# Soft-capped attention and a gated convolution on one core: sums and products with v in four groups of 32 TensorE columns, and a new order of every engine's work

## The chip, the cores and the metric

The kernel runs on one core of a Trainium2 chip. Its engines are TensorE (PE; its weight loads are listed apart as PEld), VectorE (DVE), ScalarE (ACT), GpSimd (POOL) and SyncE (SP), which here issues all DMAs. The metric is the time of one execution on the device in microseconds (us). Lower is better.

## The reference, cut to what matters

```python
# q, k, v: (8, 12, 448, 64); cap = 30
scores = (1 / sqrt(64)) * matmul(q, k.T)
scores = cap * tanh(scores / cap)
attn = exp(scores - max(scores))
attn = attn / (sum(attn) + 1e-9)
x = matmul(attn, v)                 # heads side by side: (8, 448, 768)
# gate: causal depthwise convolution of 5 taps over the sequence, per channel
gate = sigmoid(sum_k conv_w[k] * xp[:, k:k+448, :])
out = (gate * (x @ w_val)) @ w_out  # w_val, w_out: 768 x 768
```

conv_w, w_val and w_out arrive as float64, the rest as float32.

## The kernel before, in words

The 96 heads are taken as 48 pairs p; six pairs make a batch b. A pair's two heads lie on the two halves of the 128 partitions. Names of steps are those of the functions; names of tiles in brackets are those that the profile prints.

For each pair, SyncE loads q and k in blocks (qn, kn) and v (vn), and VectorE turns q and k into 64 channels by 448 positions (qt, kt; "tq", "tk"). From pair 13 on q and k are also split into a high and a low half (qh, ql, kh, kl: casts on ScalarE, subtractions on VectorE), and three matmuls of the halves take the place of one fp32 matmul. `scores` makes, for one of four chunks i of 112 keys and both heads, 112 keys by 2 x 448 queries (pss, two buffers in PSUM). `tanh` and `exp` on ScalarE make the unnormalised weights from it (pt, six buffers); no maximum is subtracted, since the cap bounds the scores. `add` on VectorE adds the four chunks up (pa): not at all before pair 6, in two pairs of chunks up to pair 10, and to one tile from pair 11 on.

Two steps then use pt. `av` (function attnv) multiplies a chunk with v: for each head 112 keys by 64 columns of v as weights and 448 queries streamed, the first head into PSUM partitions 0 to 63 and the second into 64 to 127 of one bank (psa). `sums` does the same with a tile of ones for weights (psz), so that every one of a head's 64 partitions holds the head's sum for each query. It runs once per chunk before pair 6 (four units), twice for pairs 6 to 10, once from pair 11 on: 24 + 10 + 37 = 71 units. For odd pairs below 6 both banks come from the two buffers of psf.

`turn_sums` transposes psz in 32 x 32 blocks (zt), `recip` takes one column of each block, adds a small guard and makes the reciprocals (rc), `spread` transposes them back over 32 partitions, and `mul` makes x (u, two buffers) from psa and zt. `x_hi` and `x_lo` split x (xh on ScalarE, xl on VectorE). Five `conv` steps make the gate's argument: the first is a scaled copy (on ScalarE below pair 11, on VectorE after), the others VectorE steps that each need the one before.

For each batch `sigmoid` (ScalarE) is applied to the six gates. `val` makes x @ w_val from the halves (three matmuls each, psf), `gate` multiplies, `gated_hi` and `gated_lo` split the result (g_h, g_l), and `out` makes the product with w_out, which `store` copies out of PSUM on ScalarE (osb) and `store_out` sends. In the first two batches the weights are brought from float64 into halves wv and wo, in twelve steps (weight_load, late_load, weight_first on ScalarE, weight_second and weight_third on VectorE).

The order is written out by hand. Every step is entered with a time, in units of one pair, and all are sorted by it; each engine runs its instructions in exactly that order. In the kernel before, the times come from small tables by kind of pair:

```python
"av": (1.10, 1.15, 1.20, 1.25), "sums": (1.28,), "turn_sums": 1.41, "recip": 1.42,
SIG_FIRST, SIG_AT = 6.92, 7.44          # one time for all six sigmoids of a batch
at(p + y, f, p, i)                      # a step of pair p
for _, _, f, a in sorted(events, key=lambda e: e[:2]): f(*a)
```

Tanh and exp are in one of ScalarE's function tables and the sigmoid is in another. The program loads a table (ACT_TABLE_LOAD) where the order goes from the one to the other.

The profile's lines of the kernel before that are spoken of below: scores L326, tanh L334, exp L338, add L348 and L345, av L363, sums L375, turn_sums L383, recip L389 and L390, spread L396, mul L404, x_hi L409, conv L421, L423 and L425, sigmoid L431, val L446 to L448, gate L452, gated_hi L455, out L475 to L477, store L483, turns of q and k L305, splits of weights L140 to L150, weight loads L272 and L280.

Of the kernel before, what the change touches and what calls it, by code (L numbers as in the profile page):

```python
# [7 lines left out]
F32 = mybir.dt.float32  # L8
# [32 lines left out]
STEADY = {  # L41
    "load_q": -1.9,
    "load_k": -1.85,
    "load_v": -0.6,
    "tq": -0.90,
    "tk": -0.85,
    "scores": (0.0, 0.05, 0.62, 0.67),
    "tanh": (0.06, 0.13, 0.68, 0.75),
    "exp": (0.22, 0.29, 0.82, 0.89),
    "add": (0.52, 1.03, 1.06),  # L50
    "av": (1.10, 1.15, 1.20, 1.25),
    "sums": (1.28,),
    "turn_sums": 1.41,
    "recip": 1.42,
    "spread": 1.44,
    "mul": 1.50,
    "x_hi": 1.52,
    "x_lo": 1.58,
    "conv": (1.60, 1.61, 1.64, 1.67, 1.70),
}  # L60

SPLIT = STEADY | {"q_hi": -0.69, "k_hi": -0.68, "q_lo": -0.475, "k_lo": -0.47}
PAIRED = STEADY | {"add": (0.52, 1.03), "sums": (1.28, 1.29)}
EARLY = {
    "load_q": -1.9,
    "load_k": -1.85,
    "load_v": -0.7,
    "tq": -0.72,
    "tk": -0.70,
    "scores": (-0.50, -0.49, 0.10, 0.11),  # L70
    "tanh": (0.0, 0.01, 0.35, 0.36),
    "exp": (0.17, 0.18, 0.52, 0.53),
    "av": (0.28, 0.37, 0.65, 0.80),
    "sums": (0.29, 0.38, 0.66, 0.81),
    "turn_sums": 1.02,
    "recip": 1.03,
    "spread": 1.04,
    "mul": 1.05,
    "x_hi": 1.30,
    "x_lo": 1.34,  # L80
    "conv": (1.31, 1.50, 1.52, 1.54, 1.56),
}

SIXTH = PAIRED | {k: EARLY[k] for k in ("tq", "tk", "scores", "tanh", "exp")} | {"add": (0.38, 0.62)}


TOGETHER = {
    "scores": (0.0, 0.05, 0.31, 0.32),
    "tanh": (0.06, 0.13, 0.34, 0.36),
    "exp": (0.22, 0.29, 0.47, 0.53),  # L90
    "add": (0.52, 0.60, 0.61),
}
NEXT_TOGETHER = {
    "turn_sums": 1.41, "recip": 1.42, "spread": 1.43, "mul": 1.44, "x_hi": 1.45, "x_lo": 1.54,
    "conv": (1.58, 2.16, 2.17, 2.18, 2.19),
}
PREPARE_TOGETHER = {"q_hi": -0.69, "k_hi": -0.68, "q_lo": -0.44, "k_lo": -0.43}

GATE_FIRST = {"x_lo": 1.66, "conv": (1.67, 1.68, 1.69, 1.70, 1.71)}
LATE_X = {"x_lo": 1.76, "conv": (1.78, 1.80, 1.83, 1.86, 1.89)}  # L100
NEARLY, NPAIRED, NPLAIN = 6, 11, 13

VAL_FIRST = (6.50, 6.85, 7.36, 7.74, 8.36, 8.74)
VAL = (6.85, 7.36, 7.74, 8.36, 8.74, 9.36)
SIG_FIRST, SIG_AT = 6.92, 7.44
OUT_EVEN = (9.80, 10.36, 10.74, 11.36, 11.74, 12.36)
OUT_ODD = (9.80, 10.36, 10.74, 10.80, 11.36, 11.74, 11.80, 12.36)
OUT_LATE = (9.80, 10.36, 10.74, 11.74, 12.36, 12.60)
PART = 0.13
KEEP_AT = 10.2  # L110
W_AT = (0.70, 1.70, 2.70, 3.70, 4.70, 5.70, 7.1, 8.035, 9.035, 9.7, 10.4, 11.035)
W_LOAD = -0.5
W_SECOND, W_THIRD, W_THIRD_EARLY = 0.02, 0.05, 0.71
W_FREE = 11.3
CW_LOAD, CW_AT = -0.55, 0.6
EPS = 1e-9
# [13 lines left out]
def float64_split(nc, raw, mid, hi, lo, t):  # L130

    tf = t.bitcast(F32)
    top = raw[..., 1].bitcast(F32)

    def first():
        nc.scalar.activation(tf, top, AF.Copy, scale=2.0 ** -112)  # L140
        nc.scalar.sign(top, top)

    def second():
        nc.vector.tensor_scalar(t, t, 0x0FFFFE00, 3, ALU.bitwise_and, ALU.logical_shift_left)
        nc.vector.tensor_tensor(hi, tf, top, op=ALU.mult)

    def third():
        nc.vector.tensor_scalar(mid, mid, 0x01FFFFFF, None, ALU.bitwise_and)
        nc.vector.tensor_scalar(t, hi.bitcast(I32), -0x00800000, None, ALU.bitwise_and)
        nc.vector.scalar_tensor_tensor(lo, mid, 2.0 ** -36, tf, ALU.mult, ALU.mult)  # L150

    return first, second, third
# [49 lines left out]
def fast_path(tc, io, u2, q, k, v, w_val, conv_w, w_out, out, capt):  # L202
# [20 lines left out]
    ROWS = [slice(j * D, (j + 1) * D) for j in range(2)]  # L223

    with ExitStack() as ctx:
# [24 lines left out]
        ones = cpool.tile([P, D], F32, name="ones")  # L250
# [12 lines left out]
        wstate = {}  # L263
# [11 lines left out]
        def late_load(n):  # L275
# [80 lines left out]
        def attnv(p, i):  # L356
# [5 lines left out]
            for j, r in enumerate(ROWS):  # L362
                nc.tensor.matmul(  # L363
                    st["o"][r, :S], vloads[p][:, j, i], t[:, j], start=(i == 0), stop=(i == NKT - 1)
                )

        def sums(p, i):

            st = state[p]
            n = len(tables[p]["sums"])  # L370
# [3 lines left out]
            for j, r in enumerate(ROWS):  # L374
                nc.tensor.matmul(st["z"][r, :S], ones[:CH], t[:, j], start=(i == 0), stop=(i == n - 1))  # L375
            if i == n - 1:
                vloads.pop(p)

        def turn_sums(p):
# [3 lines left out]
            nc.vector.transpose(st["zt"], st.pop("z")[:, :S])  # L383

        def norm_recip(p):
            st = state[p]
            rc = wk.tile([P, S // BLK], F32, name="rc", bufs=1)
            col = st["zt"].rearrange("p (c e) -> p c e", e=BLK)[:, :, 0]
            nc.vector.tensor_scalar(rc, col, guard, None, ALU.add)  # L389
            nc.vector.reciprocal(rc, rc)  # L390
# [16 lines left out]
        def x_hi(p):  # L407
            xh = wk.tile([P, S], F32R, name="xh", bufs=NXX)
            nc.scalar.copy(xh, gates[p][1][:, PAD:PAD + S])  # L409
# [80 lines left out]
        cw_steps = []  # L490
        events = []
        tables = [EARLY if p < NEARLY else SIXTH if p == NEARLY else PAIRED if p < NPAIRED else STEADY if p < NPLAIN else SPLIT for p in range(NP)]
        for p in range(NPAIRED, NP):
            if p % NPAIR == 0:
                tables[p] = tables[p] | LATE_X

        def together(p):
            return NPLAIN < p < NP and p % NPAIR not in (1, 3)

        for p in range(NPLAIN, NP):  # L500
            if together(p - 1):
                tables[p] = tables[p] | PREPARE_TOGETHER
            if together(p):
                tables[p] = tables[p] | TOGETHER
            if p % NPAIR == 2:
                tables[p] = tables[p] | GATE_FIRST
            if together(p + 1):
                tables[p] = tables[p] | NEXT_TOGETHER

# [13 lines left out]
        for p, table in enumerate(tables):  # L523
            for name, f in steps.items():
                x = table.get(name, ())
                if isinstance(x, tuple):
                    for i, y in enumerate(x):
                        at(p + y, f, p, i)
                else:
                    at(p + x, f, p)  # L530
        for b in range(B):
            t0 = NPAIR * b
# [207 lines left out]
```

## Time and profile before

| | |
|---|---|
| timed runs, median of 3 | 743.75 us (742.98 to 746.29) |
| span of the profiled execution | 739.6 us, first to last instruction |
| TensorE busy | 717.1 us (97%), 3972 matmul records |
| VectorE busy | 593.0 us (80%), 972 instructions |
| ScalarE busy | 534.7 us (72%), 708 instructions |
| GpSimd busy | 9.0 us (1%) |
| DMA | 63.75 MB, mean 86 GB/s |

The profiled execution's own time is its span; the timed runs also hold what lies around it. "Busy" is the time in which at least one of an engine's instructions ran. Matmuls are pipelined and one record's length includes the way through the array, so two records overlap and a busy TensorE isn't TensorE at its peak. Rows of groups read: line, engine, operation, tiles (written <- read), shapes, count | busy us, mean ns of one | idle us of the engine before them, and what ended the idle time. The granted TensorE clock was full (0.998) throughout.

### The profile page before, as it was taken

What the parts mean: (1) busy time and instruction counts of PE and PEld (TensorE: products, weight loads), DVE (VectorE), ACT (ScalarE), POOL (GpSimd) and SP (SyncE); (2) the same over time, 40 slices, a digit from 0 to 9 for tenths busy, and PEclk for the clock granted to TensorE, in tenths of its full rate; (3) what the DMA queues carried; (4) which work ended last, traced back from release to release, by engine and by line L of the source; (5) the groups of instructions that cost most, each with busy time, mean ns of one, the idle gap of its engine ahead of it and who ended that gap; (6) DMA issues with size and microseconds to landing.
All of it is one profiled execution on the core that took longest, in us unless ns stands there. A gap on an engine that the chain in (4) does not pass through costs nothing.

```text
span 739.6 us, 10858 instructions
## 1 busy us (share of the span) xinstructions
PE 717.1 (97%) x3972; PEld 488.8 (66%) x3972; DVE 593.0 (80%) x972; ACT 534.7 (72%) x708; POOL 9.0 (1%) x16
## 2 busy tenths in 40 slices
PE   5999999999999999999999999999999999999997
PEld 2333655556767776686677766757766876676997
DVE  2899999888997789988899669988899778997410
ACT  5899977787876678776957679587787659774311
POOL 0000001000000000000000000000000000000000
PEclk9999999999999999999999999999999999999999
DMA  6998867854223332224331333223322333200001
GB/s 109 223 212 209 202 171 154 225 118 80 39 49 80 74 74 38 61 67 88 57 57 47 88 75 65 39 69 74 73 38 61 70 87 57 51 24 33 23 22 68
DMA packets 241820, 63.75 MB, mean 86 GB/s; under 512 B 228448, under 2 KB 235616, under 8 KB 241760
## 3 DMA queue, kind: packets, MB, share of 16 engines
q1 hardware_dynamic: 241760, 62.98, 38.6%
q8 instruction: 33, 0.54, 0.3%
q14 instruction: 27, 0.22, 0.1%
HBM read 51.94 MB, written 11.01 MB: 85 GB/s over the span
## 4 chain that ended last, share of the span: by engine, by line
PE 52%; DVE 21%; ACT 13%; issue 2%; SPq 1%; DMA 0%; DVEq 0%; ACTq 0%
PE pss L326 9%; PE psf L475 8%; PE psf L477 7%; PE psf L476 7%; DVE gate L425 7%; PE psa L363 6%; PE psf L446 4%; PE psf L447 4%; PE psf L448 4%; ACT pt L334 3%; PE psz L375 3%; DVE pa L348 3%; ACT gate L431 3%; ACT pt L338 2%; DVE pa L345 2%
## 5 line engine op out<-in xcount | busy, mean ns | idle before, releaser
L334 ACT ACTIVATE pt<-pss,rc 112x896 f32<-112x896 f32 x192 | 185.1, 1004 | 39.2 <-PE pss L326 39.2
L338 ACT ACTIVATE pt<-pt,capt 112x896 f32<-112x896 f32 x192 | 189.6, 1041 | 0.1
L363 PE MATMUL psa<-pt,vn 112*64 112x448 f32 x720 | 147.7, 546 | 0.0
L425 DVE SCALAR_TENSOR_TENSOR gate<-u,cw,gate 128x448 f32<-128x448 f32 x192 | 130.6, 680 | 5.7
L475 PE MATMUL psf<-wo,g_h 128*128 128x384 f32 x336 | 115.7, 344 | 0.0
L477 PE MATMUL psf<-wo,g_l 128*128 128x384 f32 x336 | 112.6, 335 | 0.0
L476 PE MATMUL psf<-wo,g_h 128*128 128x384 f32 x336 | 112.4, 335 | 0.0
L446 PE MATMUL psf<-xh,wv 128*128 128x448 f32 x288 | 107.5, 373 | 0.1
L448 PE MATMUL psf<-xl,wv 128*128 128x448 f32 x288 | 104.5, 363 | 0.0
L447 PE MATMUL psf<-xh,wv 128*128 128x448 f32 x288 | 104.4, 362 | 0.0
L363 PEld LDWEIGHTS psa<-pt,vn 112*64 112x64 f32 x720 | 47.8, 136 | 81.4 <-issue 69.7
L348 DVE TENSOR_TENSOR pa<-pt 112x896 f32<-112x896 f32 x84 | 91.1, 1085 | 2.8 <-ACT pt L338 2.8
L483 ACT COPY osb<-psf 128x384 f32<-128x384 f32 x56 | 26.6, 475 | 65.3 <-PE psf L477 63.6
L383 DVE STREAM_TRANSPOSE zt<-psz 128x448 f32<-128x448 f32 x45 | 28.8, 640 | 54.2 <-PE psz L375 54.2
L475 PEld LDWEIGHTS psf<-wo,g_h 128*128 128x128 f32 x336 | 63.1, 188 | 12.3 <-issue 11.3
L446 PEld LDWEIGHTS psf<-xh,wv 128*128 128x128 f32 x288 | 54.0, 187 | 20.2 <-issue 5.4
L476 PEld LDWEIGHTS psf<-wo,g_h 128*128 128x128 f32 x336 | 63.1, 188 | 0.0
L477 PEld LDWEIGHTS psf<-wo,g_l 128*128 128x128 f32 x336 | 63.1, 188 | 0.0
L326 PE MATMUL pss<-qt,kt 64*112 64x448 f32 x208 | 49.6, 594 | 12.3 <-DVE guard L249 7.8
L455 ACT CAST g_h<-gate 128x448 fp32r<-128x448 f32 x48 | 26.3, 562 | 47.2 <-DVE gate L452 47.0
L326 PE MATMUL pss<-qh,kh 64*112 64x448 f32 x280 | 58.0, 408 | 0.0
L409 ACT CAST xh<-u 128x448 fp32r<-128x448 f32 x48 | 27.1, 566 | 42.3 <-DVE u L404 42.0
(74 smaller groups left out, 908.6 us busy)
## 6 DMA issues: line engine op xcount, KB each, us to landing
vn<-in_v_dram SPq DMA_DIRECT2D x96, 112.0 KB, 2.6
out_dram<-osb SPq DMA_DIRECT2D x56, 192.0 KB, 1.9
qn<-in_q_dram SPq DMA_DIRECT2D x188, 56.0 KB, 2.5
kn<-in_k_dram SPq DMA_DIRECT2D x188, 56.0 KB, 2.4
w_raw<-in_moe_w_val_dram SPq DMA_DIRECT2D x12, 384.0 KB, 5.1
w_late<-in_moe_w_val_dram SPq DMA_DIRECT2D x12, 384.0 KB, 4.4
w_raw<-in_moe_w_out_dram SPq DMA_DIRECT2D x12, 384.0 KB, 3.8
w_late<-in_moe_w_out_dram SPq DMA_DIRECT2D x12, 384.0 KB, 4.8
```

The source lines that it names most:

```text
L326: nc.tensor.matmul(ps[:CH, j, :S], st[x][r, c], st[y][r], start=(n == 0), stop=(n == len(parts) - 1))
L334: nc.scalar.activation(st["p", i], st.pop(("s", i)), AF.Tanh, scale=rc8[:CH])
L338: nc.scalar.activation(t, t, AF.Exp, scale=capt[:CH])
L348: nc.vector.tensor_tensor(st["a", i], st["p", 2 * i], st["p", 2 * i + 1], op=ALU.add)
L363: nc.tensor.matmul(st["o"][r, :S], vloads[p][:, j, i], t[:, j], start=(i == 0), stop=(i == NKT - 1))
L425: nc.vector.scalar_tensor_tensor(g, u[:, i:i + S], cw[:, hp, i:i + 1], g, ALU.mult, ALU.add)
L446: nc.tensor.matmul(o, w_h, xh, start=(c == 0), stop=False)
L447: nc.tensor.matmul(o, w_l, xh, start=False, stop=False)
L448: nc.tensor.matmul(o, w_h, xl, start=False, stop=(c == NCC - 1))
L475: nc.tensor.matmul(o, g_h[:, d, s], w_h, start=(d == 0), stop=False)
L476: nc.tensor.matmul(o, g_h[:, d, s], w_l, start=False, stop=False)
L477: nc.tensor.matmul(o, g_l[:, d, s], w_h, start=False, stop=(d == NCC - 1))
```

## The change

1. `av` and `sums` work in four groups of 32 TensorE columns (GROUPS) instead of two of 64. Group g serves head g // 2. In `av` each group takes 32 of the head's 64 columns of v and streams all 448 queries. In `sums` each group streams only half of the head's queries (HQ = 224): the first of a head's two groups the first half, the second the other.
2. `turn_sums` therefore transposes 224 columns instead of 448. `recip` adds the guard to 7 columns (zc) instead of 14, and makes the reciprocals in eight instructions of 32 partitions by 7, each copying one group's half to one of the head's two groups of partitions.
3. The small tables of times are replaced by large ones, one row per pair (PAIRS), batch (BLOCKS) and weight step (WEIGHTS), with a time for every step. Sigmoids get a time each. Which step runs on which engine is unchanged, and so are all other shapes and the number of buffers.

```diff
-STEADY = {
-    "load_q": -1.9,
...
+PAIRS = """
+- - -3.064 -9.09 -5.622 - - - - -4.262 -5.451 -4.05 -3.713 -3.983 -4.666 -3.924 -3.438 -3.329 -3.464 -3.153 -1.811 - -
+  - -2.746 -2.598 -1.455 -0.365 -2.81 -1.83 -1.743 -1.539 -1.354 -1.021 0.536 0.696 1.014 3.151 1.192 1.24 1.616 1.869
...
+    GROUPS = [slice(g * BLK, (g + 1) * BLK) for g in range(P // BLK)]
+    HQ = S * BLK // D
+    HC = HQ // BLK
...
-        ones = cpool.tile([P, D], F32, name="ones")
+        ones = cpool.tile([P, BLK], F32, name="ones")
...
-            for j, r in enumerate(ROWS):
+            for g, r in enumerate(GROUPS):
+                j, d = divmod(g * BLK, D)
                 nc.tensor.matmul(
-                    st["o"][r, :S], vloads[p][:, j, i], t[:, j], start=(i == 0), stop=(i == NKT - 1)
+                    st["o"][r, :S], vloads[p][:, j, i, d:d + BLK], t[:, j], start=(i == 0), stop=(i == NKT - 1)
                 )
...
-            for j, r in enumerate(ROWS):
-                nc.tensor.matmul(st["z"][r, :S], ones[:CH], t[:, j], start=(i == 0), stop=(i == n - 1))
+            for g, r in enumerate(GROUPS):
+                j, d = divmod(g * BLK, D)
+                q = slice(HQ * d // BLK, HQ * (d // BLK + 1))
+                nc.tensor.matmul(st["z"][r, :HQ], ones[:CH], t[:, j, q], start=(i == 0), stop=(i == n - 1))
...
-            nc.vector.transpose(st["zt"], st.pop("z")[:, :S])
+            nc.vector.transpose(st["zt"][:, :HQ], st.pop("z")[:, :HQ])
...
-            col = st["zt"].rearrange("p (c e) -> p c e", e=BLK)[:, :, 0]
-            nc.vector.tensor_scalar(rc, col, guard, None, ALU.add)
-            nc.vector.reciprocal(rc, rc)
+            zc = wk.tile([P, HC], F32, name="zc", bufs=1)
+            col = st["zt"].rearrange("p (c e) -> p c e", e=BLK)[:, :HC, 0]
+            nc.vector.tensor_scalar(zc, col, guard, None, ALU.add)
+            for g, r in enumerate(GROUPS):
+                j, d = divmod(g * BLK, D)
+                for x in range(D // BLK):
+                    nc.vector.reciprocal(rc[r, x * HC:(x + 1) * HC], zc[GROUPS[j * D // BLK + x]])
...
-                at(t0 + sig, sigmoid, b, d)
+                at(t0 + next(row), sigmoid, b, d)
```

What the order makes of it, at three places. Rows are an engine's instructions in the program's order, with x n for equal neighbours; the lines are each kernel's own.

TensorE around the sums of pair 18 (pss scores, psa av, psz sums), first before:

```order
L326 MATMUL pss<-qh,kl 112x448 x2
L326 MATMUL pss<-qh,kh 112x448 x2
L326 MATMUL pss<-ql,kh 112x448 x2
L326 MATMUL pss<-qh,kl 112x448 x2
L363 MATMUL psa<-pt,vn 64x448 x8
L375 MATMUL psz<-pa_2460,ones 64x448 x2
L446 MATMUL psf<-xh,wv 128x448
L447 MATMUL psf<-xh,wv 128x448
```

and now:

```order
L469 MATMUL pss<-qh,kl 112x448 x2
L507 MATMUL psa<-pt,vn 32x448 x8
L523 MATMUL psz<-pa_2831,ones 32x224 x4
L507 MATMUL psa<-pt,vn 32x448 x8
L469 MATMUL pss<-qh,kh 112x448 x2
L469 MATMUL pss<-ql,kh 112x448 x2
```

The sums moved in between two halves of av, and scores follow instead of val. Counted over the whole program, TensorE goes 210 times between full-width, two-row and column-group shapes in either order.

VectorE from the adding-up of pair 18 (L345, now L488) to its x (u), first before:

```order
L345 TENSOR_TENSOR pa_2460<-pa_2460,pa_2472 112x896
L305 STREAM_TRANSPOSE qt<-qn 128x448
L305 STREAM_TRANSPOSE kt<-kn 128x448
L425 SCALAR_TENSOR_TENSOR gate<-u_64,cw,gate 128x448 x4
L383 STREAM_TRANSPOSE zt<-psz 128x448
L389 TENSOR_SCALAR rc<-zt,guard 128x14
L390 RECIPROCAL rc<-rc 128x14
L396 STREAM_TRANSPOSE zt<-rc 128x448
L404 TENSOR_TENSOR u_63<-psa,zt 128x448
```

and now:

```order
L488 TENSOR_TENSOR pa_2831<-pa_2831,pa_2834 112x896
L575 SCALAR_TENSOR_TENSOR gate<-u_63,cw,gate 128x448
L529 STREAM_TRANSPOSE zt<-psz 128x224
L573 TENSOR_SCALAR gate<-u_64,cw 128x448
L536 TENSOR_SCALAR zc<-zt,guard 128x7
L540 RECIPROCAL rc<-zc 32x7 x8
L383 TENSOR_TENSOR xl<-u_63,xh 128x448
L383 TENSOR_TENSOR ql<-qt,qh 128x448
L546 STREAM_TRANSPOSE zt<-rc 128x448
```

Steps of other pairs now stand between the dependent steps, conv steps of two pairs alternate, and u of pair 18 comes seven rows after the last one shown. Of neighbouring conv steps that follow each other directly there are 142 before and 35 now.

ScalarE around sigmoids of the third batch (L431, now L581), first before:

```order
L311 CAST kh<-kt 128x448
L431 ACT_TABLE_LOAD
L431 ACTIVATE gate<-gate 128x448 x6
L409 CAST xh<-u_63 128x448
L334 ACTIVATE pt<-pss,rc_110 112x896
L455 CAST g_h<-gate 128x448 x2
L334 ACTIVATE pt<-pss,rc_110 112x896
L338 ACT_TABLE_LOAD
L338 ACTIVATE pt<-pt,capt 112x896 x2
```

and now:

```order
L581 ACT_TABLE_LOAD
L581 ACTIVATE gate<-gate 128x448
L477 ACTIVATE pt<-pss,rc_110 112x896 x2
L481 ACT_TABLE_LOAD
L481 ACTIVATE pt<-pt,capt 112x896 x3
L559 CAST xh<-u_63 128x448
L454 CAST qh<-qt 128x448
```

The six sigmoids of a batch moved apart, and with them the table loads: beside the one at the start there are 15 in the order before and 57 now. Between the first and the 25th tanh ScalarE has six weight steps, five x_hi and five gate copies before, and five, three and four now.

More of the change, by code (lines that the diff above doesn't have):

```diff
@@ L38 @@
 NPT = 6
-STEADY = {
-    "load_q": -1.9,
[L43 to L97, printed above, removed]
@@ L111 @@
[L111 to L115, printed above, removed]
-EPS = 1e-9
+STEPS = (
+    "load_q load_k load_v tq tk q_hi k_hi q_lo k_lo scores scores scores scores tanh tanh tanh tanh exp exp exp exp "
+    "add add add av av av av sums sums sums sums turn_sums recip spread mul x_hi x_lo conv conv conv conv conv"
+).split()
+PAIRS = """
+- - -3.064 -9.09 -5.622 - - - - -4.262 -5.451 -4.05 -3.713 -3.983 -4.666 -3.924 -3.438 -3.329 -3.464 -3.153 -1.811 - -
+  - -2.746 -2.598 -1.455 -0.365 -2.81 -1.83 -1.743 -1.539 -1.354 -1.021 0.536 0.696 1.014 3.151 1.192 1.24 1.616 1.869
+  2.29
@@ L119, in words, with plan @@
+EPS = 1e-9
+def plan(text):
+    rows = []
+    for line in text.strip("\n").split("\n"):
+        cells = [None if x == "-" else float(x) for x in line.split()]
+        if line.startswith(" "):
+            rows[-1] += cells
+        else:
+            rows.append(cells)
+    return rows
 def words(ap):
@@ L490, in fast_path @@
         cw_steps = []
+        pairs = plan(PAIRS)
+        rounds = [sum(x is not None for n, x in zip(STEPS, row) if n == "sums") for row in pairs]
         events = []
[L492 to L508, printed above, removed]
         def at(when, f, *a):
@@ L522, in fast_path @@
         )
[L523 to L532, printed above, removed]
+        for p, row in enumerate(pairs):
+            seen = {}
+            for name, when in zip(STEPS, row):
+                i = seen[name] = seen.get(name, -1) + 1
+                if when is not None:
+                    at(p + when, steps[name], p, *([i] if STEPS.count(name) > 1 else []))
@@ L552, in fast_path @@
-        for n, t0 in enumerate(W_AT):
-            third = [x + (W_THIRD if x > NEARLY else W_THIRD_EARLY) for x in W_AT]
-            at(W_AT[n - 1] + W_SECOND if n else W_LOAD, weight_load, n)
-            at(third[n - 1] if n else W_LOAD, late_load, n)
-            at(t0, weight_first, n)
-            at(t0 + W_SECOND, weight_second, n)
-            at(third[n], weight_third, n)
+                    at(t0 + next(row), val, b, d, i)
+                for f in (gate, gated_hi, gated_lo):
+                    at(t0 + next(row), f, b, d)
@@ new lines, in fast_path @@
+            for m in range(2 * (NT + b % 2)):
+                for i in range(PARTS):
+                    at(t0 + next(row), out_part, b, m, i)
+                at(t0 + next(row), store, b, m)
+                at(t0 + next(row), store_out, b, m)
+            if b % 2 == 0:
+                at(t0 + next(row), keep_tail)
+        for n, row in enumerate(plan(WEIGHTS)):
+            for f, when in zip((weight_load, late_load, weight_first, weight_second, weight_third), row):
+                at(when, f, n)
```

208 lines of the change are left out of this document (172 added, 36 removed), and 32 rows, old and new, of the table BLOCKS.

## The prediction

> **What bounds the kernel now.** I read the page first, then the groups of instructions, the timeline of TensorE around one row of av and sums steps, the busy times by stage, and last the waits. The span is 739.6 us and TensorE works nearly all of it:
>
> ```profile
> span 739.6 us, 10858 instructions
> ...
> PE 717.1 (97%) x3972; PEld 488.8 (66%) x3972; DVE 593.0 (80%) x972; ACT 534.7 (72%) x708; POOL 9.0 (1%) x16
> ```
>
> Busy shares overlap inside TensorE (matmuls are pipelined), so I price its work by the distance between starts. In the groups each fp32 matmul is two records (768 for the 384 matmuls of av in all), and the sums are 188 + 48 + 48 = 284 records:
>
> ```profile
> L363 PE MATMUL psa<-pt,vn 112*64 112x448 f32 x720 | 147.7, 546 | 0.0
> ...
> L375 PE MATMUL psz<-pa,ones 112*64 112x448 f32 x188 | 43.1, 546 | 3.8 <-DVE pa L345 3.5
> ...
> L375 PE MATMUL psz<-pt,ones 112*64 112x448 f32 x48 | 11.9, 539 | 0.0
> L375 PE MATMUL psf<-pt,ones 112*64 112x448 f32 x48 | 11.8, 539 | 0.0
> ```
>
> In the timeline (start, length, engine, records merged) eight av records take from 102.87 to 104.37, so a pair of records, one for each 64-column half of the array, costs 0.375 us; two passes make a unit (one key chunk, both heads) of 0.75 us, for av and for sums alike:
>
> ```profile
> 102.87 1.67 PE L363 MATMUL psa<-pt,vn 112*64 112x448 f32 x8
> 104.37 1.68 PE L375 MATMUL psz<-pa,ones 112*64 112x448 f32 x8
> 105.98 0.48 PE L446 MATMUL psf<-xh,wv 128*128 128x448 f32 x1
> ```
>
> The sums' eight would end their streaming at 104.37 + 4 x 0.375 = 105.87, and val starts at 105.98: a change of array shape costs 0.11 us.
>
> By stage (start:end, length, then busy us of PE, PEld, DVE, ACT, POOL; below it records of the sums line alone, PE first):
>
> ```profile
> 9.60:73.30 63.70, 61.48 (x290) 20.84 (x290) 51.92 (x93) 60.59 (x72) 0.23 (x1) 1.00 0.92 206
> 73.30:161.60 88.30, 84.77 (x420) 50.90 (x418) 81.11 (x132) 71.61 (x93) 3.14 (x2) 1.00 0.72 178
> 161.60:597.70 436.10, 433.11 (x2502) 308.92 (x2500) 373.35 (x604) 325.15 (x438) 3.46 (x4) 1.00 0.32 65
> 597.70:739.60 141.90, 135.92 (x764) 107.19 (x760) 84.72 (x137) 75.84 (x107) 1.73 (x2) 0.99 0.17 43
> ```
>
> ```profile
> 9.60:73.30 63.70, 22.96 (x94) 7.49 (x96) 1.00 0.92 206
> ```
>
> The first stage holds the first 24 tanh steps. There ScalarE is busy 60.59 of 63.70 us and TensorE 61.48: both are full, and cheaper matmuls alone can't shorten it. After 73.3 us TensorE is busy 84.77 + 433.11 + 135.92 = 653.8 of 666.3 us while VectorE (539.2) and ScalarE (472.6) have room. The waits (us in total, times, longest) say the same: ScalarE waits for scores far more than TensorE for tanh.
>
> ```profile
> ACT pt L334 <- PE pss L326: 39.2, 40, 3.8
> ...
> PE pss L326 <- ACT pt L334: 4.4, 6, 1.6
> PE psz L375 <- DVE pa L345: 3.5, 9, 0.6
> ```
>
> **Part by part.** *Sums over half the queries.* Each of the four column groups streams 224 columns instead of 448, so a pass should take 0.1875 us. Of the 284 sums records 284 - 94 = 190 lie after 73.3 us: 95 passes x 0.1875 = **17.8 us less** on the engine that sets the pace there. The 94 before it are 8.8 us of TensorE, worth nothing by themselves in a stage that ScalarE fills.
>
> *av in four groups.* Four 32-column matmuls replace two of 64, with twice the instructions and the same 448 columns each: 0.375 us a pass if four groups run side by side as two do now, so nothing. The trace shows two streams, not four. How independent they are shows where the second head's v landed late:
>
> ```profile
> 13.71 1.00 PE L363 MATMUL psa<-pt,vn 112*64 112x448 f32 x3
> 14.52 0.54 PE L375 MATMUL psz<-pt,ones 112*64 112x448 f32 x1
> 14.55 0.54 PE L363 MATMUL psa<-pt,vn 112*64 112x448 f32 x1
> ```
>
> One half is already in its sums at 14.52 while the other is still in av at 14.55, and each goes on at its own 0.375: the halves are queues of their own. I take four for the same; the other end is two at a time, doubling av (192 units x 0.75 = +144 us).
>
> *Reciprocals.* Eight of 32x7 replace one of 128x14, and the transpose ahead of them is half as wide. Prices, and how neighbours overlap on VectorE:
>
> ```profile
> L348 DVE TENSOR_TENSOR pa<-pt 112x896 f32<-112x896 f32 x84 | 91.1, 1085 | 2.8 <-ACT pt L338 2.8
> ...
> L404 DVE TENSOR_TENSOR u<-psa,zt 128x448 f32<-128x448 f32 x45 | 28.1, 624 | 1.5
> ...
> L390 DVE RECIPROCAL rc<-rc 128x14 f32<-128x14 f32 x48 | 11.6, 242 | 1.7
> ...
> L243 DVE RECIPROCAL rc<-capt 128x1 f32<-128x1 f32 x1 | 0.2, 165 | 0.7 <-DVE small L704 0.7
> ```
>
> ```profile
> 311.78 0.64 DVE L305 STREAM_TRANSPOSE qt<-qn 128x448 f32<-128x448 f32 x1
> 312.34 0.61 DVE L305 STREAM_TRANSPOSE kt<-kn 128x448 f32<-128x448 f32 x1
> ...
> 313.62 0.23 DVE L389 TENSOR_SCALAR rc<-zt,guard 128x14 f32<-128x14 f32 x1
> 313.89 0.24 DVE L390 RECIPROCAL rc<-rc 128x14 f32<-128x14 f32 x1
> ```
>
> An independent successor starts 0.08 us before its predecessor's end (312.34 against 312.42), a dependent one 0.04 after it (313.89 against 313.85). A reciprocal of seven columns lies between 165 and 242 ns, so eight take 1.32 to 1.94 us, less 7 x 0.08 = 0.56; less the old 0.24, less half a transpose (224 columns at the slope from 624 to 1085 ns for 448: 0.23). That is +0.29 to +0.91 us a pair, 14 to 44 us in all; I take 25, since seven columns are nearer one than fourteen. It is hidden: after 73.3 us VectorE idles 127 us, and the new order places other work between the dependent conv steps (142 neighbouring conv pairs before, 35 now: 107 x 0.12 = 13 us back). Uncovered, it would delay spread and mul, and through psa (one buffer) the next av.
>
> *Sigmoids.* The order sets them singly or in twos and fours between tanh and exp, where six stood together. Every such place costs two table loads: 15 beside the first before, 57 now.
>
> ```profile
> L431 ACT ACT_TABLE_LOAD x8 | 10.3, 1283 | 0.1
> L338 ACT ACT_TABLE_LOAD x7 | 9.0, 1283 | 0.1
> ```
>
> 42 x 1.283 = **53.9 us more on ScalarE**, all after 73.3 us: 472.6 becomes some 530 of 650, still below TensorE. I cost it at nothing, covered by the 39.2 us of tanh waiting for scores and other idle; the rival below has it uncovered.
>
> *First stage.* Between the first and the 25th tanh the row order before has six weight splits, five xh casts and five gate copies; the change has five, three and four. By these rows
>
> ```profile
> L409 ACT CAST xh<-u 128x448 fp32r<-128x448 f32 x48 | 27.1, 566 | 42.3 <-DVE u L404 42.0
> ...
> L141 ACT ACTIVATE w_raw<-w_raw 128x768 f32<-128x768 f32 x12 | 11.3, 943 | 0.4
> L140 ACT ACTIVATE w_t<-w_raw 128x768 f32<-128x768 f32 x12 | 11.1, 921 | 0.9 <-DMA w_raw<-in_moe_w_val_dram 0.9
> ...
> L421 ACT ACTIVATE gate<-u,cw 128x448 f32<-128x448 f32 x11 | 7.3, 666 | 0.0
> ```
>
> 0.943 + 0.921 + 2 x 0.566 + 0.666 = 3.7 us leave, less five overlaps of 0.09: **3.2 us less**. TensorE has then 61.5 - 8.8, so ScalarE stays the limit. By the same count two av units and one sums unit slip behind it: 2 x 0.75 + 0.375 = **1.9 us more** for later. On SyncE the first two weight loads go ahead of pair 1's q and k; these are wanted only after pair 0's four tanh and four exp (8 us of ScalarE), so nothing, at worst a microsecond or two.
>
> *The rest of the order.* 210 changes of array shape before and 210 now by the rows: nothing. Stalls: TensorE's waits for tanh and for the added-up tiles are 4.4 + 3.5 = 7.9 us; an order that spreads work can remove all or, with fuller ScalarE and VectorE, add. I take half off, **4.0 us less**.
>
> Sum: 739.6 - 17.8 - 3.2 + 1.9 - 4.0 = 716.5 us of span. The median of the runs shown, 743.75, lies 4.15 above the profiled span, so **720.5 us**.
>
> **Rivals.**
> *Table loads reach TensorE.* pss has two buffers, so scores i + 2 wait for tanh i; a sigmoid put ahead of that tanh delays it by two loads and itself, 3.1 us. If every load were felt the time is 720.5 + 53.9 = 774. It decides once 23.2 of the 53.9 us (43%) are felt. For it: the third batch has ten loads, and ScalarE's content there comes to 78 us by rows against 85 for TensorE. Against it: tanh mostly waits for scores, not the reverse.
>
> *Four streams are not four times one.* Each per cent that a pass of four slows costs 1.44 us in av; the forecast's gain is gone at 16%, and two at a time gives some 880. For it: no row shows four. Against it: two cost nothing. The Trainium skill's page "TensorE: Matmul & The Clock Gate" (section "Measured speedup vs the span model") lists four row tiles at 3.07 times one, and three column tiles at 2.38. By that, an estimate from the page, a pass takes 1.30 times as long and the time is about 772 us; the trace's own pairs run at a full 2 (two heads in 0.75 us), which speaks against it, and no run here shows four.
>
> *ScalarE and VectorE crowd the steady stage.* Each pair's chain of small reciprocals and the fuller ScalarE give back 10 to 19 us: 730 to 740.
>
> *More is won.* All 666.3 - 653.8 = 12.5 us without a running matmul go, instead of 4: 712; and a third of the 210 x 0.11 = 23 us of shape changes: 704.
>
> **How the numbers follow.** Chances: the forecast (712 to 730) 0.55; more is won (704 to 712) 0.13; crowding (730 to 740) 0.11; table loads 0.12, of which 0.05 end within 0.5% (740 to 747.5, about what a measurement tells from no change) and 0.07 above; four streams 0.09, all slower. Faster is 0.55 + 0.13 + 0.11 = 0.79, same 0.05, slower 0.16. The range 704 to 742 holds the first three and a little of the fourth, 0.80; the forecast's own is 712 to 730.
>
> **What would show it.** Right: sums records at 0.19 us a pass of four groups and av still at 0.375; the 25th tanh near 70 us; batches of six pairs about 2 to 3 us shorter; 57 table loads with tanh still waiting for scores. Wrong: av passes above 0.43 us; TensorE's wait for tanh grown from 4.4 to over 25 us, behind loads; mul late, with av waiting on it.

## The result, and the profile after

The changed kernel takes 733.81 us (median; 733.1 to 735.3) against 745.02 us for the kernel before in the same rounds: a ratio of 0.9865, interval 0.9837 to 0.9893. The gain is 10 to 11 us where 23 were forecast. The profiled span is 731.2 us, 8.4 below the 739.6 of before.

The page after, and then its groups by line and shape (busy us, mean ns, idle before and its releaser):

```profile
span 731.2 us, 13364 instructions
...
PE 699.2 (96%) x5024; PEld 480.1 (66%) x5024; DVE 622.2 (85%) x1308; ACT 593.3 (81%) x750; POOL 7.1 (1%) x16
```

```profile
L507 PE MATMUL psa<-pt,vn 112*32 112x448 f32 x1440 | 152.0, 544 | 2.1 <-DVE u L554 1.7
...
L540 DVE RECIPROCAL rc<-zc 32x7 f32<-32x7 f32 x384 | 73.8, 192 | 6.6
...
L581 ACT ACT_TABLE_LOAD x29 | 37.2, 1283 | 0.4
L481 ACT ACT_TABLE_LOAD x28 | 35.9, 1283 | 0.5
...
L523 PE MATMUL psz<-pa,ones 112*32 112x224 f32 x376 | 26.3, 356 | 4.6 <-DVE pa L488 3.8 <-DVE pa L491 0.7
...
L529 DVE STREAM_TRANSPOSE zt<-psz 128x224 f32<-128x224 f32 x45 | 18.2, 405 | 5.4 <-PE psz L523 5.0
```

The matmuls do what was said of them. In TensorE's timeline (start, length, records merged) 32 av records of four groups, eight passes, are followed by 16 sums records, four passes:

```profile
102.75 3.21 PE L507 MATMUL psa<-pt,vn 112*32 112x448 f32 x32
106.27 0.96 PE L523 MATMUL psz<-pa,ones 112*32 112x224 f32 x16 [0.31 <-DVE pa L491]
107.16 1.76 PE L469 MATMUL pss<-qt,kt 64*112 64x448 f32 x8
```

The last of eight passes ends 3.21 us after the first starts; a record lasts about 0.54 us, so the seven starts between take 2.67, which is 0.38 a pass. Four sums passes take 107.16 - 106.27 = 0.89 us with a change of array shape (0.11) in it, 0.19 to 0.20 a pass. Four column groups run at the pace of two.

By stage, cut at the 1st, 25th, 49th and 169th tanh as before (start:end, length, busy us of PE, PEld, DVE, ACT, POOL; then the granted TensorE clock, the DMA share and GB/s):

```profile
9.80:72.80 63.00, 56.45 (x464) 18.29 (x466) 48.40 (x117) 57.01 (x67) 0.23 (x1) 0.97 0.85 188
72.80:158.70 85.90, 81.67 (x560) 50.28 (x550) 83.14 (x170) 76.50 (x96) 1.46 (x2) 1.00 0.75 186
158.70:588.70 430.00, 422.51 (x3094) 301.67 (x3094) 395.07 (x821) 372.61 (x473) 2.72 (x4) 1.00 0.33 67
588.70:731.20 142.50, 136.67 (x916) 108.79 (x909) 93.69 (x195) 85.70 (x114) 2.30 (x2) 1.00 0.16 42
```

Against the rows of before the stages are 0.7, 2.4, 6.1 and -0.6 us shorter (with 0.2 us more ahead of them). What is new is the third number: VectorE is busy 83.14 of 85.90 us (97%) in the second stage and 395.07 of 430.00 (92%) in the third. VectorE has hardly any room left there, and TensorE's waits show it (engine and line, what it waited for, us, times, longest):

```profile
PE psz L523 <- DVE pa L488: 3.8, 5, 1.1
PE psf L507 <- DMA vn<-in_v_dram: 2.4, 1, 2.4
PE pss L469 <- ACT pt L477: 2.2, 6, 0.7
PE psf L596 <- DVE gate L602: 2.0, 2, 1.2
PE psf L596 <- DVE u L554: 1.7, 1, 1.7
PE psa L507 <- DVE u L554: 1.7, 3, 1.0
PE psf L627 <- DVE g_l L383: 1.6, 2, 1.0
```

In the waits of before, past the start-up, the added-up tiles (pa) were the only work of VectorE that TensorE waited for. Now it waits for u, gate and g_l as well.

### The profile page after: what moved, and what is told of

Its sections match the earlier page's. It is cut to its first block, busy times and chain, and to the rows that moved or that the text cites. A ratio compares the mean times of both kernels' runs of the same rounds, so it can differ in the third digit from the quotient of the medians.

```text
span 731.2 us, 13364 instructions
## 1 busy us (share of the span) xinstructions
PE 699.2 (96%) x5024; PEld 480.1 (66%) x5024; DVE 622.2 (85%) x1308; ACT 593.3 (81%) x750; POOL 7.1 (1%) x16
## 4 chain that ended last, share of the span: by engine, by line
PE 39%; DVE 26%; ACT 10%; issue 3%; DMA 2%; SPq 1%; DVEq 0%; ACTq 0%
PE psa L507 8%; PE pss L469 6%; DVE gate L575 5%; DVE pa L491 5%; PE psf L625 4%; PE psf L627 4%; PE psf L626 4%; ACT pt L481 4%; PE psf L596 3%; PE psf L598 3%; PE psf L597 3%; DVE rc L540 3%; ACT pt L477 2%; DVE pa L488 2%; ACT L481 1%
## 5 line engine op out<-in xcount | busy, mean ns | idle before, releaser
L477 ACT ACTIVATE pt<-pss,rc 112x896 f32<-112x896 f32 x192 | 188.7, 1003 | 51.3 <-PE pss L469 49.6
L481 ACT ACTIVATE pt<-pt,capt 112x896 f32<-112x896 f32 x192 | 194.9, 1042 | 1.3
L507 PE MATMUL psa<-pt,vn 112*32 112x448 f32 x1440 | 152.0, 544 | 2.1 <-DVE u L554 1.7
L575 DVE SCALAR_TENSOR_TENSOR gate<-u,cw,gate 128x448 f32<-128x448 f32 x192 | 127.5, 672 | 1.3
L491 DVE TENSOR_TENSOR pa<-pt 112x896 f32<-112x896 f32 x84 | 90.7, 1089 | 19.9 <-ACT pt L481 19.2
L507 PEld LDWEIGHTS psa<-pt,vn 112*32 112x32 f32 x1440 | 43.3, 110 | 73.2 <-issue 53.6
L540 DVE RECIPROCAL rc<-zc 32x7 f32<-32x7 f32 x384 | 73.8, 192 | 6.6
L596 PEld LDWEIGHTS psf<-xh,wv 128*128 128x128 f32 x288 | 54.0, 188 | 18.1 <-issue 5.8
L598 PEld LDWEIGHTS psf<-xl,wv 128*128 128x128 f32 x288 | 54.0, 188 | 6.8 <-DVE xl L383 1.7
L597 PEld LDWEIGHTS psf<-xh,wv 128*128 128x128 f32 x288 | 54.1, 188 | 4.6
L469 PE MATMUL pss<-ql,kh 64*112 64x448 f32 x280 | 51.6, 363 | 0.1
```

The source lines that it names most:

```text
L469: nc.tensor.matmul(ps[:CH, j, :S], st[x][r, c], st[y][r], start=(n == 0), stop=(n == len(parts) - 1))
L477: nc.scalar.activation(st["p", i], st.pop(("s", i)), AF.Tanh, scale=rc8[:CH])
L481: nc.scalar.activation(t, t, AF.Exp, scale=capt[:CH])
L491: nc.vector.tensor_tensor(st["a", i], st["p", 2 * i], st["p", 2 * i + 1], op=ALU.add)
L507: nc.tensor.matmul(st["o"][r, :S], vloads[p][:, j, i, d:d + BLK], t[:, j], start=(i == 0), stop=(i == NKT - 1))
L575: nc.vector.scalar_tensor_tensor(g, u[:, i:i + S], cw[:, hp, i:i + 1], g, ALU.mult, ALU.add)
```

## Experiments

Each kernel was timed beside the kernel before, whose median was 742.9 to 744.2 us in the four sets, so that medians are comparable within about 0.3%. Four things are in question: the order, the groups with the half-width sums, the reciprocals and the table loads. From e5 on, the runs set the order against the groups and take the reciprocals apart.

### e1: conv_w's loads on GpSimd's queue

In the first stage the row of ScalarE is 57.01 busy of 63.00 us, against 60.59 of 63.70 before: the work left, as forecast, but the time did not. The wait that took its place:

```profile
ACT cw_t L279 <- DMA cw_raw<-in_moe_conv_w_dram: 5.2, 1, 5.2
```

The five loads of conv_w are issued at 25.89 us, behind the q, k, v and weight loads that stand ahead of them on SyncE without a gap.

```diff
-CW_LOAD, CW_AT, W_FREE = -0.325, 0.739, 11.226
+CW_LOAD, CW_AT, W_FREE = -9.5, 0.739, 11.226
...
-        nc.sync.dma_start(        # conv_w
+        nc.gpsimd.dma_start(
```

> The changed kernel with the five loads of conv_w issued by GpSimd at the start instead of by SyncE behind 25 us of other issues; nothing else is moved. In the changed kernel ScalarE stood 5.2 us for them in the stage that it fills (25th tanh at 72.8 us, 3 us less work on it and no time won). Theory (the early stage lost its 3.2 us to this wait): the wait goes, the 25th tanh comes 3 to 5 us earlier, 729 to 731 us against 733.8. Rival (the stage is held by TensorE's wait for pair 1's v or by the DMA queues, so the stall only moves): within 1 us of the change.

Measured: 732.88 us (732.59 to 734.34), ratio 0.9866 (0.9846 to 0.9886), the same as the changed kernel. The wait is gone and the 25th tanh starts at 71.3 us instead of 72.8, but by the 49th the kernel is only 0.2 us ahead (158.5 against 158.7). The second stage of this profiled run:

```profile
71.30:158.50 87.20, 82.18 (x548) 50.90 (x542) 83.32 (x170) 76.52 (x97) 1.48 (x2) 0.98 0.76 180
```

The stall was real, and by the timed runs it is not worth its 5.2 us. Where the gain of the first stage goes is not shown: VectorE is busy 83.32 of 87.20 us in the second, but the granted clock was also lower there (0.98, and 1.00 in the changed kernel).

### e2: two full-width reciprocals for eight small ones

```diff
-            for g, r in enumerate(GROUPS):
-                j, d = divmod(g * BLK, D)
-                for x in range(D // BLK):
-                    nc.vector.reciprocal(rc[r, x * HC:(x + 1) * HC], zc[GROUPS[j * D // BLK + x]])
+            for x in range(D // BLK):
+                nc.vector.reciprocal(rc[:, x * HC:(x + 1) * HC], zc)
```

> The changed kernel with two reciprocals of 128x7 in place of eight of 32x7 (each group of partitions takes its own half of the queries twice, so half of the normalisers are the wrong query's; shapes and order are the same). Theory (VectorE, at 85% with 29 us more on it, is what TensorE now waits for): VectorE's busy time falls by about 6 x 0.11 x 48 = 32 us, TensorE's waits for x, gate, g_l and the added tiles fall by a third to a half, 726 to 730 us. Rival (the new order sets these waits by where it puts the steps, whatever VectorE's load): 732 to 734 us.

Measured: 720.37 us (719.04 to 723.23), ratio 0.9709 (0.9677 to 0.974). Six short operations a pair cost 13.4 us by the medians (1.56% by the ratios, 11.6). VectorE's timeline of the changed kernel, one pair:

```profile
57.80 0.23 DVE L536 TENSOR_SCALAR zc<-zt,guard 128x7 f32<-128x7 f32 x1
58.06 1.63 DVE L540 RECIPROCAL rc<-zc 32x7 f32<-32x7 f32 x8
59.72 0.65 DVE L546 STREAM_TRANSPOSE zt<-rc 128x448 f32<-128x448 f32 x1
```

and of e2, whose stages follow:

```profile
56.62 0.27 DVE L538 RECIPROCAL rc<-zc 128x7 f32<-128x7 f32 x2
```

```profile
72.40:153.60 81.20, 80.22 (x548) 50.16 (x542) 75.29 (x134) 76.30 (x97) 1.46 (x2) 1.00 0.81 195
153.60:575.60 422.00, 419.12 (x3094) 302.45 (x3094) 355.48 (x639) 372.53 (x473) 2.74 (x4) 1.00 0.33 68
575.60:718.00 142.40, 136.41 (x916) 108.97 (x910) 83.78 (x151) 85.41 (x114) 2.80 (x2) 1.00 0.16 42
```

Eight take 1.63 us, 0.204 apart, longer than one lasts (0.192): they don't overlap at all. Without the surplus VectorE's share falls to 93% and 84% in the two stages, and these are 4.7 and 8.0 us shorter. In the last stage, where VectorE was 66% busy (93.69 of 142.50), the same surplus costs 0.1 us. So the price lies in the two stages in which VectorE comes to over nine tenths, and almost none of it elsewhere.

A sum of idle time doesn't show this price. The third stage holds 30 pairs, whose surplus of 1.36 us each is 41 us; in e2 VectorE is idle for 66.5 us of that stage, more than the surplus, and in the changed kernel still for 34.9 us. But that idle time is largely VectorE's own waiting. Its longest wait over the changed kernel is for ScalarE's exps, and 11.8 us of it lie in the third stage:

```profile
DVE pa L491 <- ACT pt L481: 19.2, 14, 4.4
```

### e3: the gate as a tanh, no table loads

The sigmoid is tanh of half its argument, plus one, times a half: the one goes into the product and the half into the output's copy.

```diff
-            nc.scalar.activation(g, g, AF.Sigmoid)
+            nc.scalar.activation(g, g, AF.Tanh, scale=0.5)
...
-            nc.vector.tensor_tensor(g, psums.pop((b, d))[:, :S], g, op=ALU.mult)
+            nc.vector.scalar_tensor_tensor(g, g, 1.0, psums.pop((b, d))[:, :S], ALU.add, ALU.mult)
...
-            nc.scalar.copy(osb, psums.pop((b, "o", m))[:, :NH])
+            nc.scalar.activation(osb, psums.pop((b, "o", m))[:, :NH], AF.Copy, scale=0.5)
```

> The changed kernel with the sigmoid written as (1 + tanh(x/2))/2: tanh on ScalarE, the 1 added in the step that multiplies with the gate, the half taken in the copy out of PSUM. All 57 table loads (73 us of ScalarE) go. Theory (the loads are hidden, since tanh waits for scores 50 us in all): 731 to 734 us, no more than 3 us won. Rival (a load put ahead of a tanh or exp is felt by VectorE and TensorE through late tiles): 722 to 728 us.

Measured: 728.2 us (726.34 to 728.72), ratio 0.98 (0.9775 to 0.9826). All 57 loads between units are gone, 73 us of ScalarE, and 5.6 us come back by the medians (0.65% by the ratios, 4.8). TensorE's own wait for tanh was 2.2 us in the changed kernel, so the price doesn't stand under one name: VectorE's waits for exps fall from 19.2 to 8.3 us, and TensorE's waits for pa from 3.8 to 1.3 us. Most of the loads were hidden, as forecast. ScalarE's wait for scores, in the changed kernel and in e3, takes up 57 of the 73 us that the loads leave free:

```profile
ACT pt L477 <- PE pss L469: 49.6, 40, 4.8
```

```profile
ACT pt L477 <- PE pss L469: 106.6, 56, 5.4
```

### e4: the old order with the new groups

The kernel before, with av, sums, turn_sums and the eight reciprocals as in the change, and nothing of the new order.

```diff
-            for j, r in enumerate(ROWS):
-                nc.tensor.matmul(st["z"][r, :S], ones[:CH], t[:, j], start=(i == 0), stop=(i == n - 1))
+            for g, r in enumerate(GROUPS):
+                j, d = divmod(g * BLK, D)
+                q = slice(HQ * d // BLK, HQ * (d // BLK + 1))
+                nc.tensor.matmul(st["z"][r, :HQ], ones[:CH], t[:, j, q], start=(i == 0), stop=(i == n - 1))
...
```

> The order of the kernel before (its tables of times, word for word) with the four column groups, the half-width sums and the eight reciprocals. Theory (the groups are worth their 18 us after 73 us less what VectorE's extra 29 us cost, and the new order gives nothing back or costs some): 728 to 733 us, so at or below the whole change, the 25th tanh at 73 us as before. Rival (the new order is what makes the groups pay, the old one only turns the gain into waits for VectorE's added tiles): 736 to 744 us.

Measured: 769.97 us (768.87 to 771.97), ratio 1.0366 (1.0336 to 1.0396). What was expected of it failed: the same edit loses 27 us here. The waits of TensorE, and then of ScalarE:

```profile
PE pss L329 <- ACT pt L337: 20.5, 15, 2.3
PE psf L485 <- ACT g_h L465: 7.8, 6, 1.4
...
PE psf L456 <- DVE gate L462: 6.8, 6, 1.2
```

```profile
ACT xh L419 <- DVE u L414: 89.0, 42, 8.4
```

x_hi stands in ScalarE's queue ahead of the next tanh, and waits for u, the end of VectorE's chain from sums to mul; before, this wait was 42.0 us in 16 times. The longer chain makes x_hi wait, tanh stands behind it, and scores wait for tanh 20.5 us instead of 4.4. (The granted clock of this profiled run was 0.983; two other runs of e4, at 0.992 and 0.993, took 768.9 us, so the clock is at most a small part of the loss.)

### e5: the new order with the old groups

Two 64-column groups, full-width sums and one reciprocal in the changed kernel's order (e4's diff the other way round, on the changed kernel).

> The changed kernel's order of work, with the two 64-column groups of before for av and sums, full-width sums and one reciprocal over all 128 partitions. Theory (order and groups add up): against the kernel with two reciprocals (720.4 us) TensorE runs 192 sums passes at the length of before instead of half of it, 17.8 us more, and turn_sums is longer, so 735 to 742 us, within 1% of the kernel before. Rival A (the order alone is the gain): below 730. Rival B (the new order fits only the new lengths, as the old order fitted only the old ones, where the same edit cost 27 us): above 746. Beside it: if the two per cent on every val pass (0.205 us a slot instead of 0.201) come from where the tiles lie, they go here, since ones is 64 columns wide again and zc is gone; if they come from the order, they stay.

Measured: 733.83 us (733.46 to 734.59), ratio 0.9869 (0.9847 to 0.989). The order alone gives 10.2 us, all that the whole change gives: on top of it the groups, the shorter sums and the eight reciprocals come to nothing. The val slot is back at 0.201 us, so the order is not what slowed it.

### e6 and e7: what the eight reciprocals are slow by

e6 lets each of the eight read its own group's partitions. e7 makes the change's normalisers with five: one over all partitions, then the four whose source lies in another group.

```diff
-                    nc.vector.reciprocal(rc[r, x * HC:(x + 1) * HC], zc[GROUPS[j * D // BLK + x]])
+                    nc.vector.reciprocal(rc[r, x * HC:(x + 1) * HC], zc[r])        # e6
```

```diff
+            nc.vector.reciprocal(                                                   # e7
+                rc.rearrange("p (x c) -> p x c", c=HC), zc.unsqueeze(1).to_broadcast([P, D // BLK, HC])
+            )
             for g, r in enumerate(GROUPS):
...
-                    nc.vector.reciprocal(rc[r, x * HC:(x + 1) * HC], zc[GROUPS[j * D // BLK + x]])
+                    if x != d // BLK:
+                        nc.vector.reciprocal(rc[r, x * HC:(x + 1) * HC], zc[GROUPS[j * D // BLK + x]])
```

> The changed kernel, with each of the eight 32x7 reciprocals reading its own group's partitions instead of another group's (half of the normalisers are then those of the other queries). Theory (it is the count of short operations that costs): they stand 0.20 to 0.21 us apart as before, and the time stays at 732 to 735. Rival (reading from other partitions keeps them apart): they overlap like the two 128x7 ones, 0.12 us apart, eight take 0.95 us instead of 1.64, half of the 13.4 us that the reciprocals cost comes back, and the time is 726 to 728.

> The changed kernel with the same result from five reciprocals: one over all 128 partitions that writes both halves of rc, then the four 32x7 ones whose source lies in another group. Theory (VectorE time of the reciprocals reaches TensorE in proportion, 13.4 us for six operations more): five take about 1.05 us instead of 1.64 a pair, 0.6 of 1.36 us of the surplus goes, and the time falls by about 6 us to 727 to 729. Rival (only the first few tenths are hidden or only the last ones count): 720 to 722 or 732 to 734.

Measured: e6 722.98 us (722.01 to 723.88), ratio 0.9718 (0.9695 to 0.9742); e7 724.1 us (721.56 to 726.42), ratio 0.9723 (0.9696 to 0.975). One pair in VectorE's timeline, e6 and then e7:

```profile
56.81 1.08 DVE L540 RECIPROCAL rc<-zc 32x7 f32<-32x7 f32 x8
```

```profile
57.45 0.24 DVE L537 RECIPROCAL rc<-zc 128x14 f32<-128x14 f32 x1
57.72 0.81 DVE L544 RECIPROCAL rc<-zc 32x7 f32<-32x7 f32 x4
```

It is not the count alone. Eight that stay in their partitions take 1.08 us, 0.135 apart on the mean, and four that cross take 0.81. One by one, e6's eight alternate, as the first two show:

```profile
56.81 0.19 DVE L540 RECIPROCAL rc<-zc 32x7 f32<-32x7 f32 x1
```

```profile
56.93 0.14 DVE L540 RECIPROCAL rc<-zc 32x7 f32<-32x7 f32 x1
```

The second of a group starts 0.118 us after the first, 0.07 before that one's end; the first of the next group starts 0.013 us after the end of the one ahead. In the changed kernel each of the eight starts 0.013 after the end of the one ahead, also the four that don't cross. One rule fits all these rows: a reciprocal overlaps with the one ahead only if it reads from, and writes to, the same group of 32 partitions as that one. In e6 every second does, in the changed kernel none. It is read off these reciprocals alone, and no run tries another order of the eight. The Trainium skill's page "Vector Engine (DVE) Microarchitecture Reference", section 3.8, has it that cross-quadrant moves of a 32-partition operation are free (a quadrant is such a group). They are allowed; by these rows a change of group costs about 0.07 us of overlap.

e6 did better than its rival asked for, and e7 fell between its two. Both bursts are 0.55 us shorter a pair, and both kernels regain 10 to 11 of the 13.4 us; the next 0.8 us a pair, down to e2, is worth only 3 (about 1 by the ratios). In e6's third stage VectorE is busy 90% of the time, and the stage is 6.7 us shorter than the changed kernel's:

```profile
155.70:579.00 423.30, 419.80 (x3094) 303.09 (x3094) 380.17 (x820) 372.45 (x472) 2.73 (x4) 1.00 0.33 68
```

The price is not proportional: of the surplus over e2 the first 0.8 us a pair is hidden but for 3 us of time, and the last 0.55 costs 10.

### e8: five reciprocals and the tanh gate

> Five reciprocals as in the run above, and the gate as tanh of half its argument, with the one added in the product and the half in the output's copy, so that ScalarE loads no table between units. Theory (the two costs lie on different engines and add up): 6 us and 5.6 us under the changed kernel, 721 to 723. Rival (one wait hides the other): at the better of the two alone, 726 to 728.

Measured: 717.03 us (716.42 to 719.7), ratio 0.9651 (0.9623 to 0.968). The two gains add up: 9.7 and 5.6 off 733.8 would be 718.5. Against e7 the loads are worth 7.1 us here (5.4 by the ratios).

### e9: the old order with two reciprocals

e4 with e2's edit, to see whether its loss is the reciprocals or the groups.

> The kernel before, in its old order, with the four groups for av and sums as in the run that took 770.0 us, but with two reciprocals over all 128 partitions instead of eight over 32 (half of the normalisers are those of the other queries). Theory (the 27 us loss in the old order is the eight reciprocals alone, which stand in the chain from sums to mul that the old order gave little room): the sums' 17.8 us come through less 3.5 us on the val passes, 728 to 734 us. Rival (the old order fits nothing of the new groups, whatever the reciprocals): still above 743, at 745 to 760.

Measured: 733.49 us (732.99 to 733.75), ratio 0.9871 (0.9842 to 0.9899), at the upper end of what the theory gave. The waits of ScalarE for u:

```profile
ACT xh L417 <- DVE u L412: 37.4, 15, 6.9
```

89.0 us of e4 have gone to 37.4. The reciprocals alone cost 36.5 us in the old order and 13.4 in the new. With them out of the way the two parts stand nearly side by side (us, medians):

| | old groups, one reciprocal | new groups, two reciprocals | new groups, eight |
|---|---|---|---|
| old order | 743 to 745 | 733.5 | 770.0 |
| new order | 733.8 | 720.4 | 733.8 |

### e10: the new order, the old groups, no table loads

e5 with e3's edit.

> The new order with the old 64-column groups and one reciprocal (which took 733.8 us), and the gate as tanh, so that ScalarE loads no table between units. Theory (the table loads cost TensorE 5.6 us whatever the groups): 727 to 730 us. Rival (they cost only where VectorE is late as well): 732 to 735.

Measured: 730.99 us (730.44 to 731.91), ratio 0.9839 (0.981 to 0.9868): 2.8 us less than e5, between theory and rival. By the medians the same 57 loads cost half as much here as in the changed kernel (e3). That VectorE's room makes the difference is not shown: in e8, where VectorE also had less to do than in the changed kernel, they cost no less. Without any loads the order gives 12.6 us against the kernel before, which has 15 of its own.

### e11, e12 and e13: the val passes

Each val pass takes 0.205 us in all kernels so far with the new groups, also in the old order, and 0.201 in before, e5 and e10. In the timeline of the changed kernel:

```profile
99.84 0.37 PE L598 MATMUL psf<-xl,wv 128*128 128x448 f32 x1
100.05 0.37 PE L596 MATMUL psf<-xh,wv 128*128 128x448 f32 x1
100.25 0.37 PE L597 MATMUL psf<-xh,wv 128*128 128x448 f32 x1
100.46 0.37 PE L598 MATMUL psf<-xl,wv 128*128 128x448 f32 x1
```

864 x 0.004 = 3.5 us of TensorE. Suspect was the place of the tiles in a partition: ones is 128 bytes shorter and zc adds 32, so x_hi's tiles begin 64 bytes after a multiple of 128 instead of 32 after one. e11 makes zc 64 bytes wide in the changed kernel, e12 in e8 (x_hi's tiles 96 bytes after), and e13 restores in e8 the places of before modulo 256 bytes.

```diff
-        ones = cpool.tile([P, BLK], F32, name="ones")                 # e13 alone
+        ones = cpool.tile([P, D], F32, name="ones")[:, :BLK]
...
-            zc = wk.tile([P, HC], F32, name="zc", bufs=1)
+            zc = wk.tile([P, 16], F32, name="zc", bufs=1)[:, :HC]     # e11, e12; 64 columns in e13
```

> The changed kernel with zc laid out 64 bytes wide instead of 32 (7 of 16 columns used), so that the tiles behind it, x_hi's and gate's among them, begin 32 bytes off a multiple of 64 again, as in the kernel before; nothing else differs. Theory (the moving operand's place in SBUF makes a val pass 0.205 us instead of 0.201): the val slot falls to 0.201 and the time by up to 3.5 us, to 730 to 732. Rival (the slot depends on the groups or on the neighbours' traffic): 0.205 stays, and 733 to 735.

> Five reciprocals, the gate as tanh, and zc 64 bytes wide. Theory: 717.0 us less 3 to 3.5 us for the val passes, since TensorE waits for little there: 713 to 715. Rival (the val slot does not change): 716 to 719.

> Five reciprocals and the gate as tanh, with ones 64 columns wide and zc 256 bytes, so that wv, x_hi's and gate's tiles begin at the same places modulo 256 bytes as in the kernel before. Theory (the place of the tiles in SBUF sets the length of a val pass): the slot falls to 0.201 us in full, not spread over 0.196 to 0.213 as with zc alone padded, TensorE's 864 val passes take some 4 us less than at 0.205, and the time is 712 to 714, under the 717.0 of the unpadded kernel. Rival (the slot depends on the four groups before it, or on what VectorE and ScalarE move at the time): 0.203 to 0.205, and 714 to 717.

Measured: e11 733.69 us (732.78 to 734.72), ratio 0.9875 (0.9852 to 0.9898), nothing gained; e12 714.01 us (713.37 to 714.8), ratio 0.9605 (0.9581 to 0.9629); e13 711.83 us (710.69 to 713.66), ratio 0.9571 (0.9542 to 0.96). In e11 and e12 the slot spreads from 0.196 to 0.213 us with its median at 0.203 to 0.204; the theory of a multiple of 64 was too simple. In e13 it is back:

```profile
94.53 0.36 PE L601 MATMUL psf<-xh,wv 128*128 128x448 f32 x1
94.73 0.36 PE L602 MATMUL psf<-xl,wv 128*128 128x448 f32 x1
94.94 0.36 PE L600 MATMUL psf<-xh,wv 128*128 128x448 f32 x1
95.13 0.36 PE L601 MATMUL psf<-xh,wv 128*128 128x448 f32 x1
```

Only the places differ between e8 and e13, and 5.2 us of time with them (6 by the ratios): the place of the tiles sets the slot. By which rule, these three layouts don't tell, nor by which tile alone, since e13 moves the weights' tile (wv) back together with x_hi's. e13 leaves nothing out and is the fastest of all, 22 us below the changed kernel. Its TensorE is without a running matmul for 0.09 us in the stage from the 49th to the 169th tanh:

```profile
153.70:569.60 415.90, 415.81 (x3094) 303.84 (x3096) 379.02 (x730) 314.88 (x431) 2.74 (x4) 1.00 0.34 69
```

## Why the prediction was off

**The sign, the wide range and the matmuls held; the forecast didn't.** 733.8 lies between 704 and 742, but outside 712 to 730. It is where the rival of a crowded steady stage (730 to 740, 0.11) had it, and by what that rival named: small reciprocals (13.4 us) and a fuller ScalarE (5.6 us). That the miss is no larger is partly luck, since the order gave 5 to 7 us more than it was put at. (716.5 + 4.15 is 720.65, not 720.5; nothing hangs on it.) Sums passes at 0.19 us and av at 0.38 for four groups are as priced. The rival from the Trainium skill's page "TensorE: Matmul & The Clock Gate" (section "Measured speedup vs the span model", 3.07 times for four row tiles, 2.38 for three column tiles) doesn't hold here: four column groups give 4 times one, and none of its 52 us is seen.

**Failed: "Reciprocals", the size.** The step took 7 x 0.08 us of overlap from two transposes of all 128 partitions and reached 0.29 to 0.91 us a pair, 25 us in all. Measured is 1.63 - 0.24 - (0.640 - 0.405) = 1.16 us a pair, 55 us, outside its own range, because none of the eight overlaps with the one ahead (e2, e6).

**Failed: "Reciprocals", the cover.** "It is hidden: after 73.3 us VectorE idles 127 us" added up three stages. The prediction's own row of the second stage had VectorE busy 81.11 of 88.30 us, 92%, with 7 us to give, and 57 of the 127 (141.90 - 84.72) lay in the last stage, which could cover only its own few pairs. In the third stage the sum would have held: 62.75 us idle before, against some 35 us (30 pairs x 1.16). Yet 8.0 us were lost there (e2). Much of VectorE's idle time is its own waiting for other engines; how the surplus turned into lost time beside it, no run takes apart. This is the largest miss: 13.4 us.

**Failed: "Sigmoids", at nothing.** The 53.9 us were right by count and length (57 loads, 1.283 each), and 5.6 us of all 57 were felt (e3). ScalarE's wait for scores rose from 39.2 to 49.6 us, as a free ScalarE should show, and it covered most of the loads (e3), but not all. The rival that all are felt (774) is much further off.

**Mis-sized: "The rest of the order".** First stage, deferral and stalls were put at -3.2 + 1.9 - 4.0 = -5.3 us. The order is worth 10.2 with the table loads in it (e5) and 12.6 without any (e10). Which of its moves give this, no run takes apart. Of the 3.2 us of the first stage none came as described: the work left ScalarE, the wait for conv_w's load took its place, which the step on SyncE ("nothing, at worst a microsecond or two") had passed over, and mending it brought nothing (e1). The granted clock of this stage was 0.97 as well, and 1.00 before; what that costs is open.

**Not seen: 3.5 us of val passes** from 32 bytes of a new tile and a narrower one (by price; in e8's kernel 5.2 us were measured, with e13).

By measured terms: 743.75 - 17.8 - 12.6 + 5.6 + 13.4 + 3.5 = 735.9 us, 2 above the 733.8 measured; the terms don't quite add, as the table under e9 shows. The 17.8 and the 3.5 us stand in it by their price, and no run took the 17.8 alone: with two reciprocals, groups and sums together gave 10 to 13 us, the val passes' loss included (e9 against before; e2 against e5).

## What to carry to other kernels

An engine covers a cost only in the stage in which it has room: divide busy time by length for each stage before calling a cost hidden, and where an engine comes to over nine tenths, as VectorE did here, treat it as a second bound. Then look at what its idle time is: where it is waiting for other engines, not all of it is room. Short operations are priced by the distance between their starts in a row of the same kind, and where no such row exists, the whole length without overlap is the upper end. Take a change that loses apart before it is thrown away: the groups with the eight reciprocals cost 27 us in the old order and nothing in the new, while the groups with two reciprocals gained 10 to 13 us in either.

## Unexpected of the hardware

- Reciprocals of 32x7 in which the group of 32 partitions read or written changes from one to the next don't overlap: each starts 0.013 us after the end of the one ahead, 0.205 apart in the changed kernel and 0.151 in e6. In the same group they start 0.118 apart (e6), as two of 128x7 do (e2), with 0.07 to 0.08 us of overlap.
- A val pass of 448 columns took 0.201 or 0.205 us, or spread over 0.196 to 0.213, according to where tiles begin in the partition (e13, e8, e12); 5 to 6 us of 717 hang on it.
- 57 table loads of 1.283 us, 73 us of ScalarE, cost 2.8 us of time in one kernel (e10 against e5), 5.6 in another (e3) and 7.1 in a third (e8 against e7), by the medians.
